# Expert results in attention's output banks, the early placing one turn sooner, and VectorE's division product and choice in the next turn

## The chip, the cores and the metric

The kernel runs on one core of a Trainium2 chip. Five engines work there side by side, each on its own queue of instructions in order: PE (TensorE, matrix products into PSUM), DVE (VectorE), ACT (ScalarE), POOL (GpSimd) and SP (SyncE, which here only issues DMAs). An instruction waits on semaphores for what other engines must have done first, and while it waits, everything behind it in its queue waits too. The metric is the device time of one execution in microseconds (us); the median of three runs of the kernel before is 878.63.

## The reference, cut to what matters

Attention by clusters, and on its output a layer of experts. A query may see only the keys whose nearest centroid is its own; each token then goes to one of 8 experts.

```python
q_assign = argmax(q_n @ c_n.T);  k_assign = argmax(k_n @ c_n.T)   # 4 x 8 heads, 768 rows of 64
scores = where(q_assign == k_assign, q @ k.T / 8, -1e9)
attn = softmax(scores) @ v                       # -> x, 3072 tokens x 512
expert_idx = argmax(x_n @ emb_n.T / tau)         # 8 experts
out = gate * (relu(x @ w1[e]) @ w2[e])           # w1 512x1024, w2 1024x512, all float32
```

## The kernel before, in words

**Attention.** The work goes over 16 pairs of heads (four batches, four pairs each). A pair has 12 units (2 halves of the queries, 6 blocks of 128 keys) and is done in six turns, numbered `it` 0 to 5, of two units each. In a turn PE first makes the scores (`s_ps`, L353) of the next two units and ACT takes their exponentials (`prob`, L364); then come small pieces of work for the pair after it, or for the routing of a finished batch (`between`, L796); then PE multiplies the probabilities of this turn's two units with v into `o_ps` (L373), and DVE adds them into `acc` (L382, L392). Six units make a group with one `o_ps` and one `acc`. A turn after a group's last unit, that is at `it` 0 and 3, `total` has PE sum `acc` over the keys (L400) and ACT copy the sum to `den`; `divide` has DVE take the reciprocal (L416) and multiply `o_ps` by it into `xT` (L417).

The mask is made for the next pair: at `it` 2 `assign` finds each row's largest centroid product (`amax`, `sel`), POOL weighs `sel` (L276), and `choose` makes of it the one-hot rows `oh` (`pm` L282, `oh` L283). At `it` 4 PE turns these, and DVE copies the queries' part to `qH` (L302), ACT the keys' part to `kH`. The next pair's scores, from `it` 5 on, read both.

**Experts.** Tokens are sorted by expert into blocks of 128 rows. The first four blocks are placed early, from the first three batches, while the last batch's attention runs: `Places` works in the steps `ranks`, `firsts`, `experts`, `dest`, `hot_blocks`, `hot_rows` and `tokens`, and the table `early` (L780) says in which turn each is done; `(3, 4)` is `it` 4 of the batch's last pair. After `tokens`, POOL gathers a block's rows (`fetch`, L693, an indirect DMA into `xin`). A block j is then done in three steps: `turn_x` (PE transposes into `x_ps`, L723, copied to `xTm` by ACT or DVE, L725), `hidden` (PE into `h_ps`, L737, ACT to `hT`, L744) and `result` (PE into `y_ps`, L753, ACT scales it to `y`, L763, POOL scatters it to the output, L764). `weights` has SP load an expert's two matrices where the expert changes.

**Order.** Attention and the first blocks are in `manual_schedule`: PE, DVE and ACT do there what the program says, in its order. The loop over the later blocks (L921) is ordered by the framework, which puts one product of block j's `result` between the transposes of block j+1 and that block's `hidden`. PSUM has eight banks: two for `o_ps`, two for `misc`, four for `s_ps`; these four become one `x_ps`, two `h_ps` and one `y_ps` when attention is over.

Of the kernel before, what the change touches and what calls it, by code (L numbers as in the profile page):

```python
# [9 lines left out]
F32 = mybir.dt.float32  # L10
# [8 lines left out]
P = 128  # L19
# [18 lines left out]
def kernel(  # L38
# [83 lines left out]
    ldp = at.enter_context(tc.tile_pool(name="ldp", bufs=2, side="right"))  # L122
    trp = at.enter_context(tc.tile_pool(name="trp", bufs=2, side="right"))
    pp = at.enter_context(tc.tile_pool(name="pp", bufs=5, side="right"))
    psS = at.enter_context(tc.tile_pool(name="psS", bufs=2, space=PSUM, side="right"))

# [98 lines left out]
    def prep_pieces(n):  # L227
# [89 lines left out]
        def mean(bk):  # L317
# [12 lines left out]
            "turn1": lambda: (turn("q", 1), turn("k", 1)),  # L330
            "values": values,
            "products": products,
            "assign": lambda: (assign(), choose()),
            "hots": lambda: (turn_hot(0, "q"), turn_hot(1, "k")),
        }

# [1 line left out]
    GU = NJ  # L338
# [56 lines left out]
    def total(g):  # L395

        d = gr[g]
        bk = misc()
        for h in range(2):
            nc.tensor.matmul(  # L400
                bk[D * h : D * h + D, 0:HS],
                lhsT=ones,
                rhs=d["acc"][:, h],
                start=True,
                stop=True,
            )
        d["den"] = smp.tile([P, HS], F32, tag="den", name="den")
        nc.scalar.copy(d["den"], bk[:, 0:HS])  # L408

    def divide(g):  # L410
        n, hq, _ = units[GU * g]
        b, hp = pairs[n]
        d = gr[g]
        if (b, hq) not in xT:
            xT[b, hq] = xp.tile([P, NHP, HS], F32, tag="xT", name="xT", bufs=3)
        nc.vector.reciprocal(d["den"], d["den"])  # L416
        nc.vector.scalar_tensor_tensor(  # L417
            out=xT[b, hq][:, hp],
            in0=d["o_ps"][:, 0:HS],
            scalar=ld[n]["ev"],  # L420
            in1=d["den"],
            op0=ALU.add,
            op1=ALU.mult,
        )
        d.clear()
# [290 lines left out]
            cond=c > 0,  # L716
        )

    def turn_x(j, evict):
        d = mo[j]  # L720
        bk = psX.tile([P, DM], F32, tag="x_ps", name="x_ps")
        for c in range(KD):
            nc.tensor.transpose(bk[:, P * c : P * c + P], d["xin"][:, P * c : P * c + P], ident)  # L723
        d["xT"] = mop.tile([P, DM], F32, tag="xTm", name="xTm")
        evict(d["xT"], bk)  # L725

    def hidden(j, halves=(0, 1)):
# [18 lines left out]
    def result(j, halves=(0, 1)):  # L746
        d = mo[j]
        for half in halves:
            if half == 0:
                d["y_ps"] = psY.tile([P, DM], F32, tag="y_ps", name="y_ps")  # L750
            bk = d["y_ps"]
            for c in range(KF // 2 * half, KF // 2 * half + KF // 2):
                nc.tensor.matmul(  # L753
                    bk,
                    lhsT=d["hT"][:, P * c : P * c + P],
                    rhs=w2s[j % 2][:, c],
                    start=(c == 0),
                    stop=(c == KF - 1),
                )
            if half == 1:  # L760
                to = gidxs[0][:, j : j + 1] if j < KA else sidx[:, j - KA : j - KA + 1]
                y = mop.tile([P, DM], F32, tag="y", name="y", bufs=3)
                nc.scalar.activation(y, bk, ACTF.Copy, scale=d["xin"][:, DM : DM + 1])  # L763
                nc.gpsimd.indirect_dma_start(  # L764
                    out=out[:],
                    out_offset=bass.IndirectOffsetOnAxis(ap=to, axis=0),
                    in_=y,
                    in_offset=None,
                    bounds_check=N - 1,
                    oob_is_err=False,  # L770
                )
                del mo[j]
# [6 lines left out]
    pa = Places(0, rta)  # L779
    early = {  # L780
        (2, 3): lambda: pa.ranks(),
        (2, 5): lambda: (pa.firsts(), pa.experts()),
        (3, 0): lambda: pa.dest(),
        (3, 1): lambda: (pa.hot_blocks(), pa.hot_rows(0, 3)),
        (3, 2): lambda: pa.hot_rows(1, 3),
        (3, 3): lambda: pa.hot_rows(2, 3),
        (3, 4): lambda: (pa.tokens(), fetch(0), fetch(1), fetch(2)),
    }

    def piece(n, name):  # L790
# [5 lines left out]
    def between(n, it):  # L796
        b, nb = divmod(n, NHP)
        if it == 5:
            piece(n + 2, "turn0")
            if n + 1 == NP:  # L800
                route[b] = route_pieces(b)
                rows(2 * n)
                route[b][0](0)
        elif it == 0:
            piece(n + 1, "turn1" if n else "turn0")
        elif it == 1:
            piece(n + 1, "values")
            piece(n + 1, "products")
            if n > 0:
                rows(2 * n - 2)  # L810
        elif it == 2:
            piece(n + 1, "assign")
            if n > 0:
                rows(2 * n - 1)
        elif it == 4:
            piece(n + 1, "hots")
        if b > 0:
            if nb == 0 and it == 3:
                route[b - 1] = route_pieces(b - 1)
                for half in range(2):  # L820
                    route[b - 1][0](half)
            j = NJ * nb + it - 3
            if 0 <= j < NJ:
                route[b - 1][2](j)
            if nb == 1 and it == 3:
                for half in range(2):
                    route[b - 1][1](half)
            if nb in (1, 2) and 0 <= j - NJ < 4:
                route[b - 1][3][j - NJ]()
        if b == B - 1 and (nb, it) in early:  # L830
            early[nb, it]()
        if b == B - 1 and (nb, it) == (3, 0):
            weights(0)
            weights(1)

    with tc.manual_schedule(engines={EngineType.PE, EngineType.DVE, EngineType.Activation}):
        for name in ("turn0", "turn1", "values", "products", "assign", "hots"):
            piece(0, name)
        load(1, "qk")
        for m in range(2):  # L840
            scores(m)
            expo(m)
        for i in range(0, len(units), 2):
            n, it = divmod(i // 2, NJ)
            if it == 0 and n + 1 < NP:
                load(n + 1, "v")
            if it == 4 and n + 2 < NP:
                load(n + 2, "qk")
            if it == 0 and n == 1:

                for w in range(2):
                    nc.sync.dma_start(
                        out=w1s[w], in_=moe_w1[0].rearrange("(c p) f -> p c f", p=P)
                    )
                    nc.sync.dma_start(
                        out=w2s[w], in_=moe_w2[0].rearrange("(c p) d -> p c d", p=P)
                    )
            for m in range(i + 2, min(i + 4, len(units))):
                scores(m)
                expo(m)  # L860
            between(n, it)
            for m in range(i, i + 2):
                attend(m)
            if i % GU == 0 and i > 0:
                total(i // GU - 1)
                divide(i // GU - 1)
            if i == 0:
                piece(1, "turn1")
        at.close()
        tile_waits = {"side": "right", "reuse_waits": "tile"}  # L870
        mop = ctx.enter_context(tc.tile_pool(name="mop", bufs=2, **tile_waits))
        rtb = ctx.enter_context(tc.tile_pool(name="rtb", bufs=1, **tile_waits))
        psX, psH, psY = (
            ctx.enter_context(tc.tile_pool(name=name, bufs=bufs, space=PSUM, **tile_waits))
            for name, bufs in (("psX", 1), ("psH", 2), ("psY", 1))
        )

        products, logits, norms, (choose, *gates) = route[B - 1]
        pb = Places(1, rtb)
        turn_x(0, nc.scalar.copy)  # L880
        hidden(0, (0,))
        total(ngroups - 1)
        divide(ngroups - 1)
        for j in range(NJ // 2):
            norms(j)
        hidden(0, (1,))
        turn_x(1, nc.scalar.copy)
        logits(0)
        rows(ngroups - 1)
        products(1)  # L890
        hidden(1, (0,))
        for j in range(NJ // 2, NJ):
            norms(j)
        logits(1)
        choose()
        hidden(1, (1,))
        for gate in gates:
            gate()
        fetch(3)
        turn_x(2, nc.scalar.copy)  # L900
        result(0, (0,))
        pb.ranks()
        pb.firsts()
        result(0, (1,))
        weights(2)
        pb.dest()
        pb.experts()
        hidden(2)
        pb.hot_blocks()
        turn_x(3, nc.scalar.copy)  # L910
        pb.hot_rows(0, 1)
        result(1)
        weights(3)
        hidden(3, (0,))
        pb.tokens()
        hidden(3, (1,))
# [72 lines left out]
```

## Time and profile before

| | |
|---|---|
| runs | 878.63 us median (878.53 to 878.80) |
| profiled execution | 881.44 us, span 879.6 us, clock granted to PE 0.989 of full speed |
| PE | busy 834.4 us, 95% of the span |
| DVE / ACT / POOL | 357.2 / 305.2 / 117.4 us busy |
| attention | until about 440 us of the span |
| experts | from there to 870 us, 28 blocks; a block takes 15.06 us |

PE is hardly ever idle, so what counts is what PE waits for; the other engines' idle time means nothing by itself. A bracket at a row's end gives the idle time of that engine just before the row, and what ended it. PE's matmuls of float32 stand in the trace as two records each (x4 for two matmuls), and their ends are modelled: from start to start is the safer measure.

### The profile page before, as it was taken

Reading aid. Unit: us, or ns where it says so; the run is one execution under the profiler, and the core shown is the slowest. Engines: PE = TensorE matmul, PEld = TensorE weight load, DVE = VectorE, ACT = ScalarE, POOL = GpSimd, SP = SyncE. Lnnn points to the kernel's source line nnn. Section 1 sums busy time; section 2 is a strip of 40 time slices with the busy share of each in tenths; the row PEclk is TensorE's granted clock in tenths of the full one; section 3 lists DMA queues with packets and bytes.
Section 4 is the critical chain, followed back from the end, with each engine's and each line's share of the span. In section 5 each row is a group of like instructions: output and inputs, shape, how many; then the busy total and the mean of one; then the engine's idle time right before and its main releaser. Section 6 shows DMA issues by size and latency. Waiting matters only on the chain.

```text
span 879.6 us, 12823 instructions
## 1 busy us (share of the span) xinstructions
PE 834.4 (95%) x5227; PEld 496.4 (56%) x5227; DVE 357.2 (41%) x521; ACT 305.2 (35%) x489; POOL 117.4 (13%) x172
## 2 busy tenths in 40 slices
PE   4999999999999999999989999999999999999995
PEld 2444444444444444444376676767676767767672
DVE  3477777777778777788925000000000000000000
ACT  3455555755566545665432111111111111111110
POOL 4010101210102111111011101011010101010100
PEclk8899999999999999999999999999999999999998
DMA  9922201242201422001037756838383847216400
GB/s 239 324 55 55 53 19 37 56 126 55 54 19 37 126 54 55 19 19 73 1 132 272 275 195 231 303 128 322 120 314 136 290 160 271 86 61 241 173 29 21
DMA packets 108781, 115.24 MB, mean 131 GB/s; under 512 B 77221, under 2 KB 77221, under 8 KB 108208
## 3 DMA queue, kind: packets, MB, share of 16 engines
q1 hardware_dynamic: 104064, 100.68, 35.6%
q0 software_dynamic: 4480, 13.65, 4.1%
q8 instruction: 43, 0.70, 0.3%
q14 instruction: 18, 0.15, 0.1%
q10 hardware_dynamic: 176, 0.05, 0.0%
HBM read 152.11 MB, written 13.64 MB: 188 GB/s over the span
## 4 chain that ended last, share of the span: by engine, by line
PE 32%; issue 31%; DMA 21%; DVE 12%; POOL 2%; ACT 1%; SPq 0%; POOLq 0%; DVEq 0%
DMA out_dram<-y,sidx 16%; PE s_ps L353 13%; PE o_ps L373 8%; DVE den L416 4%; PE misc L238 3%; DMA out_dram<-y,gidx 3%; DVE acc L392 2%; PE misc L400 2%; PE h_ps L737 2%; POOL sel L276 1%; PE misc L253 1%; DMA xin<-x_rows,gidx 1%; DVE xT L417 1%; PE misc L434 1%; PE misc L266 1%
## 5 line engine op out<-in xcount | busy, mean ns | idle before, releaser
L737 PEld LDWEIGHTS h_ps<-xTm,w1s 128*128 128x128 f32 x1792 | 205.9, 193 | 15.2 <-DVE xTm L725 7.2
L753 PE MATMUL y_ps<-w2s,hT 128*128 128x512 f32 x448 | 203.6, 598 | 8.9 <-ACT y L763 8.9
L737 PE MATMUL h_ps<-xTm,w1s 128*128 128x128 f32 x1792 | 207.2, 277 | 0.7 <-ACT xTm L725 0.7
L364 ACT ACTIVATE prob<-s_ps 128x768 f32<-128x768 f32 x192 | 154.6, 811 | 140.6 <-PE s_ps L353 81.4
L353 PE MATMUL s_ps<-qT,kT 64*128 64x384 f32 x768 | 157.8, 489 | 0.0
L725 DVE COPY xTm<-x_ps 128x512 f32<-128x512 f32 x24 | 16.6, 692 | 340.8 <-PE x_ps L723 340.8
L373 PE MATMUL o_ps<-prob,v 128*64 128x384 f32 x768 | 145.1, 499 | 0.0
L753 PEld LDWEIGHTS y_ps<-w2s,hT 128*128 128x128 f32 x448 | 81.0, 190 | 97.2 <-issue 81.7
L392 DVE TENSOR_TENSOR acc<-acc,prob 128x768 f32<-128x768 f32 x128 | 122.1, 954 | 3.6
L744 ACT ACTIVATE hT<-h_ps 128x512 f32<-128x512 f32 x56 | 33.4, 597 | 209.2 <-PE h_ps L737 209.2
L416 DVE RECIPROCAL den<-den 128x384 f32<-128x384 f32 x32 | 81.7, 2552 | 33.1 <-ACT den L408 33.1
L353 PEld LDWEIGHTS s_ps<-qT,kT 64*128 64x128 f32 x768 | 70.1, 192 | 21.9 <-issue 21.9
L373 PEld LDWEIGHTS o_ps<-prob,v 128*64 128x64 f32 x768 | 46.6, 136 | 54.4 <-issue 53.4
L763 ACT ACTIVATE y<-y_ps,xin 128x512 f32<-128x512 f32 x28 | 19.2, 687 | 154.8 <-PE y_ps L753 142.6
L353 PE MATMUL s_ps<-qH,kH 64*128 64x384 bf16 x384 | 64.6, 331 | 6.5 <-DVE qH L302 5.3
L764 POOL DMA_INDIRECT out_dram<-y,sidx x24 | 24.0, 1001 | 300.8 <-ACT y L763 293.9
L353 PEld LDWEIGHTS <-kH 64*128 64x128 bf16 x384 | 20.6, 94 | 75.5 <-issue 52.9
L312 POOL TENSOR_TENSOR vs<-v 128x384 f32<-128x384 f32 x16 | 16.5, 1030 | 222.1 <-DMA v<-in_v_dram 222.1
L693 POOL DMA_INDIRECT xin<-x_rows,gidx x28 | 30.2, 1078 | 31.4 <-issue 11.2
L247 DVE COPY kT<-misc 128x384 f32<-128x384 f32 x32 | 17.8, 558 | 40.6 <-PE misc L238 40.2
L400 PE MATMUL misc<-acc,ones 128*64 128x384 f32 x128 | 26.7, 493 | 4.9 <-DVE acc L392 4.9
L382 DVE SCALAR_TENSOR_TENSOR acc<-prob 128x768 f32<-128x768 f32 x32 | 30.3, 948 | 0.0
(183 smaller groups left out, 487.2 us busy)
## 6 DMA issues: line engine op xcount, KB each, us to landing
w1s<-in_moe_w_dram SPq DMA_DIRECT2D x30, 2048.0 KB
w2s<-in_moe_w_dram SPq DMA_DIRECT2D x30, 2048.0 KB
x_rows<-xr SPq DMA_DIRECT2D x4, 1539.0 KB
q<-in_q_dram SPq DMA_DIRECT2D x32, 192.0 KB
k<-in_k_dram SPq DMA_DIRECT2D x32, 192.0 KB
v<-in_v_dram SPq DMA_DIRECT2D x32, 192.0 KB
xin<-x_rows,gidx POOLq DMA_INDIRECT x28, 7.2
out_dram<-y,sidx POOLq DMA_INDIRECT x24, 6.9
```

The lines of the kernel that those rows point to most:

```text
L238: nc.tensor.transpose(bk[:, P * j : P * j + P], t[nm][:, NJ // 2 * half + j].rearrange("p h d -> p (h d)"), ident,)
L353: nc.tensor.matmul(s_ps[:, h, 0:HS], lhsT=t[l][rows, P * j : P * j + P], rhs=t[r][rows, HS * hq : HS * hq + HS], start=first, stop=not first,)
L364: nc.scalar.activation(d["prob"], d["s_ps"][:, :, 0:HS], ACTF.Exp)
L373: nc.tensor.matmul(g["o_ps"][D * h : D * h + D, 0:HS], lhsT=ld[n]["v"][:, j, h], rhs=d["prob"][:, h], start=(j == 0), stop=(j == NJ - 1),)
L382: nc.vector.scalar_tensor_tensor(out=g["acc"], in0=un[i - 1]["prob"], scalar=NJ * EPS, in1=d["prob"], op0=ALU.add, op1=ALU.add,)
L392: nc.vector.tensor_tensor(g["acc"], g["acc"], d["prob"], ALU.add)
L400: nc.tensor.matmul(bk[D * h : D * h + D, 0:HS], lhsT=ones, rhs=d["acc"][:, h], start=True, stop=True,)
L416: nc.vector.reciprocal(d["den"], d["den"])
L693: nc.gpsimd.indirect_dma_start(out=xin, out_offset=None, in_=x_rows[0:n], in_offset=bass.IndirectOffsetOnAxis(ap=gidxs[part][:, c : c + 1] ...
L737: nc.tensor.matmul(bk[:, m : m + P], lhsT=w1s[j % 2][:, c, f0 + m : f0 + m + P], rhs=d["xT"][:, P * c : P * c + P], start=(c == 0), stop=( ...
L744: nc.scalar.activation(d["hT"][:, f0 : f0 + 512], bk, ACTF.Relu)
L753: nc.tensor.matmul(bk, lhsT=d["hT"][:, P * c : P * c + P], rhs=w2s[j % 2][:, c], start=(c == 0), stop=(c == KF - 1),)
```

## The change

Four things are moved.

The results go into the two `o_ps` banks, which attention has left by then, in turns; `y_ps` has no bank of its own, and `h_ps` gets three. For that `psS` is closed one turn earlier, and the transposes of block 0 move ahead of attention's last two units, with `xTm` in a buffer of `acc`.

The reciprocal moves from `divide` to `total`, where it comes as before, and the rest of `divide` moves to the next turn, behind that turn's pieces and ahead of its additions. `choose` moves from `it` 2 to `it` 3. The early steps from `firsts` on come a turn sooner. In block 1's `result` the transposes of block 3 move between its two halves.

```diff
-            "assign": lambda: (assign(), choose()),
+            "assign": assign,
+            "choose": choose,
...
         nc.scalar.copy(d["den"], bk[:, 0:HS])
+        nc.vector.reciprocal(d["den"], d["den"])
...
-        nc.vector.reciprocal(d["den"], d["den"])
...
-                d["y_ps"] = psY.tile([P, DM], F32, tag="y_ps", name="y_ps")
+                d["y_ps"] = psO.tile([P, DM], F32, tag="o_ps", name="y_ps")
...
-        (2, 5): lambda: (pa.firsts(), pa.experts()),
-        (3, 0): lambda: pa.dest(),
...
-        (3, 4): lambda: (pa.tokens(), fetch(0), fetch(1), fetch(2)),
+        (2, 4): lambda: (pa.firsts(), pa.experts()),
+        (2, 5): lambda: pa.dest(),
...
+        (3, 3): lambda: (pa.tokens(), fetch(0), fetch(1), fetch(2)),
...
+        elif it == 3:
+            piece(n + 1, "choose")
...
             between(n, it)
+            if i % GU == 2 and i > GU:
+                divide(i // GU - 1)
+            if i + 2 == len(units):
+                ats.close()
...
+                turn_x(0, nc.scalar.copy, xp.tile([P, DM], F32, tag="acc", name="xTm"))
...
                 total(i // GU - 1)
-                divide(i // GU - 1)
...
-        turn_x(0, nc.scalar.copy)
...
+        pb.hot_rows(0, 1)
+        result(1, (0,))
         turn_x(3, nc.scalar.copy)
-        pb.hot_rows(0, 1)
-        result(1)
+        result(1, (1,))
```

On DVE, in a pair of the first batch, `it` 2 to 4 stood in this order before (`acc` x2 are a turn's two additions):

```order
L274 TENSOR_REDUCE amax<-misc 128x24
L275 TENSOR_TENSOR sel<-misc,amax 128x384
L282 TENSOR_REDUCE pm<-sel 128x24
L283 TENSOR_TENSOR oh_176<-sel,pm 128x24x16
L392 TENSOR_TENSOR acc<-acc,prob 128x768 x2
L382 SCALAR_TENSOR_TENSOR acc<-prob 128x768
L416 RECIPROCAL den<-den 128x384
L417 SCALAR_TENSOR_TENSOR xT<-o_ps,ev,den 128x384
L302 TENSOR_SCALAR qH<-misc 128x768
L306 COPY ev<-misc 128x1
```

And there now:

```order
L275 TENSOR_REDUCE amax<-misc 128x24
L276 TENSOR_TENSOR sel<-misc,amax 128x384
L394 TENSOR_TENSOR acc<-acc,prob 128x768 x2
L283 TENSOR_REDUCE pm<-sel 128x24
L284 TENSOR_TENSOR oh_176<-sel,pm 128x24x16
L384 SCALAR_TENSOR_TENSOR acc<-prob 128x768
L411 RECIPROCAL den<-den 128x384
L303 TENSOR_SCALAR qH<-misc 128x768
L307 COPY ev<-misc 128x1
L419 SCALAR_TENSOR_TENSOR xT<-o_ps,ev,den 128x384
```

The two additions have moved ahead of the choice, and the product `xT` behind `qH`.

On DVE too, the end of the step `dest` in the last batch and what followed it, before:

```order
L637 CAST blka<-blkfa 128x18
L638 SCALAR_TENSOR_TENSOR loa<-blkfa,desta 128x18
L382 SCALAR_TENSOR_TENSOR acc<-prob 128x768
L416 RECIPROCAL den<-den 128x384
L417 SCALAR_TENSOR_TENSOR xT<-o_ps,ev,den 128x384
```

And now:

```order
L639 CAST blka<-blkfa 128x18
L640 SCALAR_TENSOR_TENSOR loa<-blkfa,desta 128x18
L394 TENSOR_TENSOR acc<-acc,prob 128x768 x2
L650 TENSOR_TENSOR bma<-io_b,blka 128x72
L652 TENSOR_TENSOR rra<-bma,tok_hi 128x18x4
```

The two additions that complete a group's `acc`, which were ahead of all of `dest`, now stand behind it.

On PE, the last turn of attention and the first block, before:

```order
L434 MATMUL misc<-ident,xT 128x128 x3
L456 MATMUL misc<-xT,embT 32x384 x4
L373 MATMUL o_ps<-prob,v_3584 64x384 x4
L723 MATMUL x_ps<-ident,xin 128x128 x4
L737 MATMUL h_ps<-xTm,w1s_58 128x128 x16
```

And now:

```order
L436 MATMUL misc<-ident,xT 128x128 x3
L458 MATMUL misc<-xT,embT 32x384 x4
L725 MATMUL x_ps<-ident,xin 128x128 x4
L375 MATMUL o_ps<-prob,v_3584 64x384 x4
L739 MATMUL h_ps<-xTm,w1s_58 128x128 x16
```

The transposes `x_ps` have moved ahead of the last products with v. In the loop over blocks PE's order is the same as before; the banks alone differ.

## Rows read from the trace of the kernel before

**Rows 1.** The page: busy us, share of the span and instructions, by engine

```profile
PE 834.4 (95%) x5227; PEld 496.4 (56%) x5227; DVE 357.2 (41%) x521; ACT 305.2 (35%) x489; POOL 117.4 (13%) x172
```

**Rows 2.** PE's waits over the whole span: us in total, times, longest

```profile
PE y_ps L753 <- ACT y L763: 8.9, 25, 0.8
PE s_ps L353 <- DVE qH L302: 5.3, 15, 0.8
PE misc L400 <- DVE acc L392: 4.9, 10, 0.7
PE x_ps L723 <- DMA xin<-x_rows,gidx: 3.1, 2, 2.0
```

**Rows 3.** Timeline of PE, half a pair: start us, us, instruction, idle before

```profile
222.55 1.51 PE L373 MATMUL o_ps<-prob,v 128*64 128x384 f32 x8
224.56 0.87 PE L400 MATMUL misc<-acc,ones 128*64 128x384 f32 x4 [0.50 <-DVE acc L392]
225.36 0.34 PE L353 MATMUL s_ps<-qH,kH 64*128 64x384 bf16 x2
...
229.78 0.34 PE L353 MATMUL s_ps<-qH,kH 64*128 64x384 bf16 x2 [0.24 <-DVE qH L302]
...
236.28 1.51 PE L373 MATMUL o_ps<-prob,v 128*64 128x384 f32 x8
...
238.36 0.34 PE L353 MATMUL s_ps<-qH,kH 64*128 64x384 bf16 x2
```

**Rows 4.** Timeline of DVE, the same pair and the next one's choice

```profile
225.98 2.55 DVE L416 RECIPROCAL den<-den 128x384 f32<-128x384 f32 x1 [0.69 <-ACT den L408]
228.65 0.62 DVE L417 SCALAR_TENSOR_TENSOR xT<-o_ps,ev,den 128x384 f32<-128x384 f32 x1
229.18 0.55 DVE L302 TENSOR_SCALAR qH<-misc 128x768 bf16<-128x768 bf16 x1
...
247.26 0.55 DVE L282 TENSOR_REDUCE pm<-sel 128x24 bf16<-128x384 bf16 x1 [1.02 <-POOL sel L276]
...
248.33 2.01 DVE L392 TENSOR_TENSOR acc<-acc,prob 128x768 f32<-128x768 f32 x2
```

**Rows 5.** Timeline of PE, a turn of the loop over blocks

```profile
621.53 0.60 PE L723 MATMUL x_ps<-ident,xin 128*128 128x128 f32 x4
622.47 1.13 PE L753 MATMUL y_ps<-w2s,hT 128*128 128x512 f32 x2 [0.34 <-ACT y L763]
623.43 7.31 PE L737 MATMUL h_ps<-xTm,w1s 128*128 128x128 f32 x64
630.58 6.17 PE L753 MATMUL y_ps<-w2s,hT 128*128 128x512 f32 x14
```

**Rows 6.** Timeline of DVE, the same turn

```profile
622.17 0.69 DVE L725 COPY xTm<-x_ps 128x512 f32<-128x512 f32 x1 [14.37 <-PE x_ps L723]
```

**Rows 7.** Timeline of DVE, additions, first of the twelve of `dest`, next after them

```profile
417.44 1.93 DVE L392 TENSOR_TENSOR acc<-acc,prob 128x768 f32<-128x768 f32 x2
419.29 0.30 DVE L614 TENSOR_TENSOR wa<-rka,offa 128x144 f32<-128x144 f32 x1
...
422.09 0.95 DVE L382 SCALAR_TENSOR_TENSOR acc<-prob 128x768 f32<-128x768 f32 x1
```

**Rows 8.** Timeline of PE, the last pair and the first block

```profile
420.05 0.81 PE L400 MATMUL misc<-acc,ones 128*64 128x384 f32 x4
...
442.08 0.63 PE L723 MATMUL x_ps<-ident,xin 128*128 128x128 f32 x4 [1.98 <-DMA xin<-x_rows,gidx]
443.39 5.37 PE L737 MATMUL h_ps<-xTm,w1s 128*128 128x128 f32 x32 [0.68 <-ACT xTm L725]
...
449.48 3.84 PE L737 MATMUL h_ps<-xTm,w1s 128*128 128x128 f32 x32
```

**Rows 9.** Timeline of POOL, the first gather

```profile
437.97 1.67 POOL L693 DMA_INDIRECT xin<-x_rows,gidx  x1 [11.17 <-DVE gidx L678]
```

**Rows 10.** Stretches: us, busy time by engine, granted clock of PE, DMA share, GB/s

```profile
443.40:445.00 1.60, 1.60 (x7) 1.60 (x8) 0.00 (x0) 0.00 (x0) 0.00 (x0) 0.50 0.55 169
```

More of the change, by code (lines that the diff above doesn't have):

```diff
@@ L124 @@
     pp = at.enter_context(tc.tile_pool(name="pp", bufs=5, side="right"))
-    psS = at.enter_context(tc.tile_pool(name="psS", bufs=2, space=PSUM, side="right"))
+    ats = ctx.enter_context(ExitStack())
+    psS = ats.enter_context(tc.tile_pool(name="psS", bufs=2, space=PSUM, side="right"))
     def misc():
@@ L717, in weights, with turn_x @@
         )
-    def turn_x(j, evict):
+    def turn_x(j, evict, xT=None):
         d = mo[j]
@@ L723, in turn_x @@
             nc.tensor.transpose(bk[:, P * c : P * c + P], d["xin"][:, P * c : P * c + P], ident)
-        d["xT"] = mop.tile([P, DM], F32, tag="xTm", name="xTm")
+        d["xT"] = mop.tile([P, DM], F32, tag="xTm", name="xTm") if xT is None else xT
         evict(d["xT"], bk)
@@ L781 @@
         (2, 3): lambda: pa.ranks(),
-        (2, 5): lambda: (pa.firsts(), pa.experts()),
-        (3, 0): lambda: pa.dest(),
-        (3, 1): lambda: (pa.hot_blocks(), pa.hot_rows(0, 3)),
-        (3, 2): lambda: pa.hot_rows(1, 3),
-        (3, 3): lambda: pa.hot_rows(2, 3),
-        (3, 4): lambda: (pa.tokens(), fetch(0), fetch(1), fetch(2)),
+        (2, 4): lambda: (pa.firsts(), pa.experts()),
+        (2, 5): lambda: pa.dest(),
+        (3, 0): lambda: (pa.hot_blocks(), pa.hot_rows(0, 3)),
+        (3, 1): lambda: pa.hot_rows(1, 3),
+        (3, 2): lambda: pa.hot_rows(2, 3),
+        (3, 3): lambda: (pa.tokens(), fetch(0), fetch(1), fetch(2)),
     }
@@ L836 @@
     with tc.manual_schedule(engines={EngineType.PE, EngineType.DVE, EngineType.Activation}):
-        for name in ("turn0", "turn1", "values", "products", "assign", "hots"):
+        for name in ("turn0", "turn1", "values", "products", "assign", "choose", "hots"):
             piece(0, name)
@@ L861 @@
             between(n, it)
+            if i % GU == 2 and i > GU:
+                divide(i // GU - 1)
+            if i + 2 == len(units):
+                ats.close()
+                tile_waits = {"side": "right", "reuse_waits": "tile"}
+                psX = ctx.enter_context(tc.tile_pool(name="psX", bufs=1, space=PSUM, **tile_waits))
+                turn_x(0, nc.scalar.copy, xp.tile([P, DM], F32, tag="acc", name="xTm"))
             for m in range(i, i + 2):
@@ L869 @@
         at.close()
-        tile_waits = {"side": "right", "reuse_waits": "tile"}
         mop = ctx.enter_context(tc.tile_pool(name="mop", bufs=2, **tile_waits))
         rtb = ctx.enter_context(tc.tile_pool(name="rtb", bufs=1, **tile_waits))
[L873 to L876, printed above, removed]
+        psH = ctx.enter_context(tc.tile_pool(name="psH", bufs=3, space=PSUM, **tile_waits))
         products, logits, norms, (choose, *gates) = route[B - 1]
         pb = Places(1, rtb)
-        turn_x(0, nc.scalar.copy)
         hidden(0, (0,))
```

## The prediction

> **What bounds the kernel now.** I read the page first [rows 1]: PE is busy for 834.4 of 879.6 us, so time can come only from PE's idle 45 us and from PE working slowly. Next the list of PE's waits [rows 2]. Four of its lines are touched by the change: results waiting for ACT's copy of the result before (8.9 us), scores waiting for `qH` (5.3), sums waiting for `acc` (4.9), transposes waiting for a gather (3.1); 22.2 us in all. The reader should see that these are many small waits, of 0.24 to 0.8, in every pair and every block. Then the timelines, to see what a wait costs beside its idle time and what is late next: a pair [rows 3, 4], a turn of the loop [rows 5, 6], and the passage from attention to the experts [rows 7 to 10].
>
> The sum is made against the profiled execution's own 881.44 us, which is 2.8 above the median of 878.63; I take each gain off either.
>
> **Attention.** The instructions are the same; DVE's order changes.
>
> At `it` 2 the additions stood behind the choice, and that behind POOL's product: DVE sat 1.02 us idle before `pm`, and the choice's `pm` and `oh` take 1.07, from 247.26 to 248.33 [rows 4]. With the additions ahead of them, they end 2.1 us sooner. PE's sum L400 waited 0.5 for them [rows 3], 0.7 at most [rows 2]. So all ten of these waits go. A wait of 0.50 costs more than that: from the products at 222.55 to the next scores at 225.36 it is 2.81 us, without the wait 2.08 (236.28 to 238.36), so 0.73, of which 0.23 is PE starting again. Ten times: 4.9 + 2.3 = 7.2 us.
>
> The choice now stands in the turn of the reciprocal. That costs nothing while DVE reaches the reciprocal before `den` does: there is 0.69 idle before the reciprocal [rows 4], and DVE comes 1.02 sooner, because the wait for POOL is now filled with additions. PE comes 0.73 sooner, which leaves about 1.0 of slack. PE reads `oh` only at `it` 4, behind that turn's scores.
>
> `qH` stood behind the product `xT`, which takes 0.53 from start to next start (228.65 to 229.18 [rows 4]). It now comes first, 0.53 sooner against waits that average 0.24 in most pairs (the 229.78 row of [rows 3] is one). In the few with 0.8, where the routing fills DVE, 0.53 is not enough by itself, but part of POOL's 1.02 comes on top. All 5.3 go; I add nothing for starting again. The product comes after `qH`, a turn before PE turns `xT`, so nobody waits for it in a plain pair; the `o_ps` bank that it frees is written again two turns on. Attention: 7.2 + 5.3 = 12.5 us. From below: 9, if another copy (`kH` by ACT stands at the same gate) is late in some pairs; from above 13.5, if each `qH` wait cost 0.07 more.
>
> **The loop over blocks.** In each turn PE does four transposes, one product of the last block's result and then `hidden`. That product waits 0.34 for ACT to empty the one bank; with two banks the other has been empty for a whole turn. From transposes to `hidden` it is 1.90 us (621.53 to 623.43 [rows 5]). What is late next? First the product itself: it could start at 0.94 - 0.34 = 0.60 after the transposes, and its two records take 0.44 each (6.17 us for 14), so it ends at 1.48. Then `xTm`: DVE's copy ends at 622.17 + 0.69, which is 1.33 after the transposes' start [rows 6]; add some 0.15 until PE has taken it, an estimate from the 0.1 that PE loses on starting again in [rows 5] (0.96 from the product's start to `hidden`, against 0.88). Both come out at 1.48 to 1.49, so 0.41 a turn. The 25 waits are 24 of 0.34 and one of 0.8: 24 x 0.41 = 9.8 us, and 0.8 for the last block, where nothing follows but its own result. From below 24 x 0.2 = 4.8, if PE takes `xTm` as late as 1.7; from above 24 x 0.5 = 12, if neither is felt.
>
> The Trainium skill speaks against this term: its page "TensorE: Matmul & The Clock Gate", section "HAM oscillation — how this bites in real kernels", reports of a matmul kernel that "Adding PSUM double-buffering gave no further gain". By it the loop would give 0 in place of 10.6, and the sum would be 15.2. The row bears the other way: here the bank is the wait that ends last, 0.34 each time.
>
> **The passage.** Before, PE stood 1.98 us for the first gather and 0.68 for `xTm`, and then ran half of `hidden` in 5.37 us in place of 3.84, the granted clock being at its lower level, 0.50 (1.2 of 2.4 GHz) [rows 8, 10]. The gather is issued at 437.97 and lands with the transposes' start at 442.08 [rows 9, 8]. Its whole chain now comes a turn sooner (4.4 us from 225.36 to 229.78 [rows 3]), past no other work of POOL or SP, and `xTm` is copied beside the last products with v. So 1.98 + 0.68 + 1.53 = 4.2 us would go.
>
> Against that stands a new wait. The two additions that complete a group now come behind the twelve instructions of `dest`, 2.80 us (419.29 to 422.09 [rows 7]). They ended at 419.29; they will end there + 2.80, less what DVE is ahead by then (0 to 1.0 of POOL's wait; I take 0.35, because the reciprocal between is held by `den`): about 421.75. PE's L400 stood at 420.05 [rows 8]; it comes sooner by the waits gone ahead of it in this pair, 0.4 to 1.0 by their kinds in [rows 2, 3]; I take 0.65, so 419.4. PE waits 2.35 there, and 0.23 for starting again: 2.6 us (1.7 to 3.3). Behind L400 on PE are the next scores, so ACT's exponentials and DVE's reciprocal come later too; DVE is the fuller engine here, and the transposes of the last `xT` may wait some 0.7 for the product that now comes a turn later. Short waits of that size leave in this stretch too; I let them cancel. If the clock falls after the new wait as it did after the old ones, another 1.5 is lost; I don't count it, but the range does. Passage: 4.2 - 2.6 = 1.6 us, from -0.5 to 4.2.
>
> **Block 3.** The second gather wait is 3.1 - 1.98 = 1.1 us [rows 2, 8]; half of block 1's result now stands ahead of the transposes, eight records of 0.44, so the gather is hidden. 1.1 us; 0 if the weights that SP loads for block 3 are late instead.
>
> Three `h_ps` banks in place of two: nothing; the list of PE's waits has none for `h_ps` to be emptied.
>
> **The sum.** 12.5 + 9.8 + 0.8 + 1.6 + 1.1 = 25.8 us: 855.6 for an execution like the profiled one, 852.8 for the median.
>
> **The rivals.**
>
> *The loop gives nothing.* `hidden` can't start before `xTm`, and the product was beside DVE's copy anyway; or the product's start still waits for ACT, for `hT`. For: copy and product end within 0.1 of each other. Against: today `hidden` starts 0.57 after the copy's end (1.33 to 1.90), so the copy does not set it; and `hT` was copied a turn earlier. Time: 852.8 + 10.6 = 863.4.
>
> *Attention gives half.* DVE's work is the same, and PE, coming sooner, meets `kH` or the exponentials late. For: `prob` has five buffers that DVE's additions free. Against: additions come sooner, not later. Time: 852.8 + 6.2 = 859.0.
>
> *Slower: the choice holds up the reciprocal in every pair.* If the additions at `it` 2 didn't come sooner, 1.07 us of choice would stand between them and the reciprocal, and `qH` would be later by as much. Then the sum loses attention's 12.5, and 1.07 x 16 = 17 more is spent, and the passage's 1.6 goes: 25.8 - 12.5 - 17 - 1.6 = -5.3, so 884. It decides from where attention loses (9.8 + 0.8 + 1.1) / 16 = 0.73 us a pair. Against: the reciprocal has 0.69 of idle time ahead of it today, and the additions read probabilities made a turn before.
>
> *It doesn't do what it says.* The sums then wait for something else at the same time, and the loop for `xTm` as long as for the bank: 878.
>
> **How the numbers follow.** Forecast 0.79, its own range 848 to 859. Loop nothing 0.10, attention half 0.06, slower 0.03, no change 0.02. The lows of the terms together (9 + 4.8 + 0.8 - 0.5 + 0) give 864.5, the highs (13.5 + 12 + 1 + 4.2 + 1.1) 846.8; all ends together are unlikely, but the first rival lies near the low one: 847 to 863. A measurement here tells 0.2% (1.8 us) from no change. Faster: 0.95; same 0.02; slower 0.03.
>
> **What would show it.** Right: no waits of L400 for `acc` but one, of 1.4 to 3 us, in the turn after `dest`; none of scores for `qH` or under 0.2 in some pairs; loop turns of 14.65 us in place of 15.06, with `hidden` waiting for DVE's `xTm`; no wait for a gather at either place; the first half of `hidden` in 3.8 us. Wrong: turns of 15.06, `qH` waits that grow, or a long stretch at the granted clock 0.50 after the new wait, which would make the passage a loss.

## The result and the profile after

The changed kernel takes 856.77 us (median of four runs, 855.87 to 857.99), against 878.71 of the kernel before beside it: a ratio of 0.9745, interval 0.9725 to 0.9766. The forecast was 852.8, its range 847 to 863. The profiled execution took 857.06 us, its span 855.3. Lines have moved: L353 is now L355, L392 L394, L400 L402, L417 L419, L434 L436, L723 L725, L737 L739, L753 L755; the reciprocal is L411.

The page's busy row, against [rows 1], and the list of PE's waits, against [rows 2]:

```profile
PE 828.1 (97%) x5227; PEld 491.2 (57%) x5227; DVE 362.5 (42%) x521; ACT 305.5 (36%) x489; POOL 126.5 (15%) x172
```

```profile
PE h_ps L739 <- DMA w1s<-in_moe_w_dram: 2.8, 5, 0.7
PE misc L402 <- DVE acc L394: 2.2, 1, 2.2
...
PE misc L436 <- DVE xT L419: 0.7, 1, 0.7
```

All four lines of [rows 2] are gone, but for one wait of L402. Two lines are new: `hidden` waits five times for the load of w1, and one transpose waits for `xT`. DVE and POOL are busier with the same instructions.

PE in the half pair of [rows 3], and DVE's reciprocal in it, as [rows 4]:

```profile
214.98 1.51 PE L375 MATMUL o_ps<-prob,v 128*64 128x384 f32 x8
216.32 0.82 PE L402 MATMUL misc<-acc,ones 128*64 128x384 f32 x4
217.06 0.34 PE L355 MATMUL s_ps<-qH,kH 64*128 64x384 bf16 x2
...
221.17 0.34 PE L355 MATMUL s_ps<-qH,kH 64*128 64x384 bf16 x2
```

```profile
217.69 2.55 DVE L411 RECIPROCAL den<-den 128x384 f32<-128x384 f32 x1 [0.57 <-ACT den L410]
```

From products to the next scores it is now 2.08 us (2.81 before), and neither the sum nor the scores at 221.17 wait. DVE still reaches the reciprocal 0.57 before `den` does.

PE in two turns of the loop, as [rows 5], and DVE in the first:

```profile
618.63 0.60 PE L725 MATMUL x_ps<-ident,xin 128*128 128x128 f32 x4
619.07 1.02 PE L755 MATMUL y_ps<-w2s,hT 128*128 128x512 f32 x2
620.02 7.41 PE L739 MATMUL h_ps<-xTm,w1s 128*128 128x128 f32 x64
627.27 6.17 PE L755 MATMUL y_ps<-w2s,hT 128*128 128x512 f32 x14
633.28 0.60 PE L725 MATMUL x_ps<-ident,xin 128*128 128x128 f32 x4
633.71 1.02 PE L755 MATMUL y_ps<-w2s,hT 128*128 128x512 f32 x2
635.33 7.38 PE L739 MATMUL h_ps<-xTm,w1s 128*128 128x128 f32 x64 [0.59 <-DMA w1s<-in_moe_w_dram]
```

```profile
619.27 0.69 DVE L727 COPY xTm<-x_ps 128x512 f32<-128x512 f32 x1 [13.95 <-PE x_ps L725]
```

A turn takes 14.65 (618.63 to 633.28; 15.06 before): the product follows the transposes after 0.44 and `hidden` after 1.39 (620.02), not 1.90, 0.06 behind the end of DVE's copy (619.96). From the start of `hidden` to that of `result` it is 7.25 (7.15 before), so 0.10 of the 0.51 goes again. In the next turn `hidden` comes after 2.05, because w1 is late.

DVE and PE behind `dest`, against [rows 7, 8]:

```profile
403.96 0.30 DVE L616 TENSOR_TENSOR wa<-rka,offa 128x144 f32<-128x144 f32 x1
...
406.75 1.95 DVE L394 TENSOR_TENSOR acc<-acc,prob 128x768 f32<-128x768 f32 x2
```

```profile
408.75 0.87 PE L402 MATMUL misc<-acc,ones 128*64 128x384 f32 x4 [2.17 <-DVE acc L394]
409.55 0.34 PE L355 MATMUL s_ps<-qH,kH 64*128 64x384 bf16 x2
409.73 1.37 PE L355 MATMUL s_ps<-qT,kT 64*128 64x384 f32 x4
...
429.99 3.84 PE L739 MATMUL h_ps<-xTm,w1s 128*128 128x128 f32 x32
```

And the stretch behind that wait, columns as [rows 10]:

```profile
409.60:413.30 3.70, 3.70 (x17) 1.67 (x15) 3.70 (x3) 1.84 (x3) 0.00 (x0) 0.54 0.00 0
```

PE waits 2.17, and then the granted clock falls to its lower level (1.2 of 2.4 GHz; 0.54 is the mean of this stretch, the fall included): the scores at 409.73 take 1.37 where 0.81 is usual. `hidden`'s first half takes 3.84, no longer 5.37 [rows 8].

**Where the time came from.** PE's instructions are the same in all kernels here, so I cut each profiled execution at the starts of the same five of them: the first, the 27th and the last of the 32 sums of `acc`, the transposes of block 4, and the span's end. Differences of two starts in the PE timeline, us:

| kernel | head | attention, pairs 1 to 13 | passage | blocks 0 to 3 | loop | span |
|---|---|---|---|---|---|---|
| before | 41.71 | 340.61 | 66.37 | 52.15 | 378.76 | 879.6 |
| changed | 39.83 | 330.33 | 63.60 | 51.60 | 369.94 | 855.3 |
| changed, second profile | 40.16 | 330.33 | 61.95 | 51.75 | 369.51 | 853.7 |
| b_choose | 39.83 | 334.37 | 66.85 | 52.00 | 378.55 | 871.6 |
| b_divide | 40.77 | 335.75 | 62.78 | 52.56 | 378.64 | 870.5 |
| b_attn | 39.43 | 330.33 | 62.20 | 52.20 | 378.54 | 862.7 |
| b_loop | 41.65 | 340.66 | 66.36 | 52.37 | 370.16 | 871.2 |
| a_place | 39.84 | 330.34 | 62.20 | 51.75 | 369.57 | 853.7 |
| a_tab | 40.57 | 330.33 | 64.57 | 51.91 | 369.22 | 856.6 |
| a_dest | 39.59 | 330.33 | 63.66 | 51.80 | 370.52 | 855.9 |
| a_w1 | 40.29 | 330.33 | 63.54 | 50.81 | 367.43 | 852.4 |
| a_dest_w1 | 39.92 | 330.33 | 62.03 | 50.81 | 367.51 | 850.6 |
| a_best | 40.22 | 330.33 | 62.38 | 50.81 | 367.46 | 851.2 |
| a_pool | 38.62 | 330.33 | 63.60 | 51.85 | 369.30 | 853.7 |

Before to changed: 1.9 + 10.3 + 2.8 + 0.55 + 8.8 = 24.3 us. Between kernels with the same order there, attention's column differs by 0.05 at most, so it says what a median can't; the head (38.6 to 40.6 with attention changed) and the loop with its waits for w1 (369.2 to 370.5) repeat less well.

### The profile page after: what moved, and what is told of

Read it like the earlier page. It is cut to its first block, busy times and chain, and to the rows that moved or that the text cites. A ratio compares the mean times of both kernels' runs of the same rounds, so it can differ in the third digit from the quotient of the medians.

```text
span 855.3 us, 12807 instructions
## 1 busy us (share of the span) xinstructions
PE 828.1 (97%) x5227; PEld 491.2 (57%) x5227; DVE 362.5 (42%) x521; ACT 305.5 (36%) x489; POOL 126.5 (15%) x172
## 4 chain that ended last, share of the span: by engine, by line
PE 49%; issue 25%; DMA 22%; DVE 2%; SPq 0%; POOL 0%; ACT 0%; POOLq 0%
PE s_ps L355 19%; DMA out_dram<-y,sidx 17%; PE o_ps L375 16%; PE misc L239 3%; DMA out_dram<-y,gidx 3%; PE misc L402 2%; PE h_ps L739 2%; DMA w1s<-in_moe_w_dram 2%; PE misc L436 2%; PE misc L297 1%; PE misc L254 1%; PE misc L267 1%; PE y_ps L755 1%; PE misc L458 1%; DVE den L411 1%
## 5 line engine op out<-in xcount | busy, mean ns | idle before, releaser
L739 PEld LDWEIGHTS h_ps<-xTm,w1s 128*128 128x128 f32 x1792 | 202.5, 192 | 24.2 <-DVE xTm L727 20.5
L739 PE MATMUL h_ps<-xTm,w1s 128*128 128x128 f32 x1792 | 207.9, 277 | 2.8 <-DMA w1s<-in_moe_w_dram 2.8
L755 PE MATMUL y_ps<-w2s,hT 128*128 128x512 f32 x448 | 201.1, 592 | 0.0
L355 PE MATMUL s_ps<-qT,kT 64*128 64x384 f32 x768 | 157.7, 489 | 0.0
L394 DVE TENSOR_TENSOR acc<-acc,prob 128x768 f32<-128x768 f32 x128 | 129.8, 1014 | 3.6
L755 PEld LDWEIGHTS y_ps<-w2s,hT 128*128 128x128 f32 x448 | 81.0, 190 | 81.8 <-issue 81.8
L411 DVE RECIPROCAL den<-den 128x384 f32<-128x384 f32 x32 | 81.7, 2552 | 31.2 <-ACT den L410 31.2
L355 PEld LDWEIGHTS s_ps<-qT,kT 64*128 64x128 f32 x768 | 69.6, 191 | 22.1 <-issue 22.1
L355 PE MATMUL s_ps<-qH,kH 64*128 64x384 bf16 x384 | 64.1, 331 | 1.0 <-ACT kH L306 0.9
L355 PEld LDWEIGHTS <-kH 64*128 64x128 bf16 x384 | 19.0, 94 | 70.8 <-issue 48.2
L277 POOL TENSOR_TENSOR sel<-sel,prefc 128x384 bf16<-128x384 bf16 x16 | 24.2, 1514 | 110.2 <-DVE sel L276 110.2
```

The costliest lines, as they stand in the source:

```text
L277: nc.gpsimd.tensor_tensor(sel, sel, bc(prefc, shp, 1), ALU.mult)
L355: nc.tensor.matmul(s_ps[:, h, 0:HS], lhsT=t[l][rows, P * j : P * j + P], rhs=t[r][rows, HS * hq : HS * hq + HS], start=first, stop=not first,)
L394: nc.vector.tensor_tensor(g["acc"], g["acc"], d["prob"], ALU.add)
L739: nc.tensor.matmul(bk[:, m : m + P], lhsT=w1s[j % 2][:, c, f0 + m : f0 + m + P], rhs=d["xT"][:, P * c : P * c + P], start=(c == 0), stop=( ...
L755: nc.tensor.matmul(bk, lhsT=d["hT"][:, P * c : P * c + P], rhs=w2s[j % 2][:, c], start=(c == 0), stop=(c == KF - 1),)
```

## The experiments

**One part alone, on the kernel before.** `b_loop`: the banks of the results.

```diff
-                d["y_ps"] = psY.tile([P, DM], F32, tag="y_ps", name="y_ps")
+                d["y_ps"] = psO.tile([P, DM], F32, tag="o_ps", name="y_ps")
...
-            for name, bufs in (("psX", 1), ("psH", 2), ("psY", 1))
+            for name, bufs in (("psX", 1), ("psH", 3))
```

> The kernel before with one part of the change alone: the results go into attention's two output banks, and h_ps has three. Theory (the loop's new bound is the weight loads): each turn saves 0.41 us (24 x 0.41 = 9.8) and the last block 0.8, and four turns that follow two weight loads give back 0.66 each, 2.6: 8.0 us, about 870.7; the list of PE's waits has four of hidden for w1s, of 0.3 to 0.7. Rival 1 (the weight waits of the changed kernel come from the other parts): 10.6 us, 868.1, no such waits. Rival 2 (the loop gives nothing): 878.7.

872.14 us against 881.17, ratio 0.9902 (0.9886 to 0.9917); the loop column falls by 8.6. PE's list:

```profile
PE h_ps L737 <- DMA w1s<-in_moe_w_dram: 2.5, 5, 0.7
```

The waits for weights come with the shorter turn, not with the other parts. Five of them, not four: block 4 waits here too (0.38), where in the changed kernel block 3 does. The third `h_ps` bank came along and wasn't run apart; PE's list of before has no wait for `h_ps` to be emptied.

`b_attn` has all of attention's part, `b_choose` the first of these two edits, `b_divide` the second:

```diff
-            "assign": lambda: (assign(), choose()),
+            "assign": assign,
+            "choose": choose,
...
+        elif it == 3:
+            piece(n + 1, "choose")
...
```

```diff
         nc.scalar.copy(d["den"], bk[:, 0:HS])
+        nc.vector.reciprocal(d["den"], d["den"])
...
+            if i % GU == 2 and i > GU:
+                divide(i // GU - 1)
...
-                divide(i // GU - 1)
```

> The kernel before with attention's part of the change alone: the choice in the next turn, the reciprocal in total, the product xT in the next turn; places, transposes and results as before. Theory: the ten waits of sums for acc (7.2 us) and the fifteen of scores for qH (5.3 us) go, 12.5 us: 866.2. Rival (part of it comes from the early placing): 10 us or less, over 868.5, with waits for qH or acc left in the last batch.

> The kernel before with only the choice moved from it 2 to it 3. Theory: the ten waits for acc go with what PE loses on starting again, 7.2 us: 871.5; the fifteen waits for qH stay as they are, 5.3 us. Rival (starting again costs nothing, only the idle time comes back): 4.9 us, 873.8. Rival (the choice delays the reciprocal): the waits for qH grow to 10 us or more, gain under 3 us.

> The kernel before with only division changed: reciprocal in total, product xT in the next turn. Theory: the fifteen waits for qH go, 5.3 us and nothing for starting again: 873.4; the ten waits for acc stay, 4.9 us. Rival (each such wait costs 0.07 to 0.23 more than its idle time, as the waits for acc did): 6.4 to 8.8 us, 870 to 872.3. Rival (the product ahead of the additions delays the sums): waits for acc grow by 0.5 each, no gain.

Measured: 865.58 (0.9829, 0.9816 to 0.9843), 872.95 (0.9912, 0.9898 to 0.9925), 872.26 (0.9906, 0.9892 to 0.9920), all against 881.17: 15.1, 7.8 and 8.3 us by the ratios (15.6, 8.2 and 8.9 from median to median). The lists of PE's waits, of `b_choose` and of `b_divide`:

```profile
PE s_ps L354 <- DVE qH L302: 3.3, 14, 0.3
PE x_ps L724 <- DMA xin<-x_rows,gidx: 3.0, 2, 2.0
...
PE misc L401 <- DVE acc L393: 0.4, 1, 0.4
```

```profile
PE misc L400 <- DVE acc L392: 4.5, 9, 0.7
...
PE x_ps L723 <- DMA xin<-x_rows,gidx: 2.2, 2, 1.6
PE misc L434 <- DVE xT L417: 1.9, 2, 1.4
```

Each edit removes its own waits. In pairs 1 to 13 there are seven waits for `acc` behind the first sum and thirteen for `qH` (3.5 and 4.3 us). The choice's edit gains 6.24 there: 3.5, 1.1 of the `qH` waits, and 1.6 for starting again, 0.23 a wait. Division's gains 4.86, 0.04 a wait above the idle time. So `acc` waits cost 0.23 more than they show, `qH` waits hardly anything, as the prediction had it. `b_attn` gains more than 12.5 for a reason that wasn't in the expectation: the passage column falls by 4.17, and `b_divide` alone does 3.59 of it. Its gather waits 0.64 instead of 1.98 and the first half of `hidden` takes 3.84, with the old table:

```profile
434.23 0.63 PE L723 MATMUL x_ps<-ident,xin 128*128 128x128 f32 x4 [0.64 <-DMA xin<-x_rows,gidx]
435.54 3.84 PE L737 MATMUL h_ps<-xTm,w1s 128*128 128x128 f32 x32 [0.68 <-ACT xTm L725]
```

(The 1.6 in its list is the second gather, of block 3.) `b_choose` leaves the first gather's wait as it was (2.0), and its passage column is 0.48 longer than before: that half of `hidden` takes 6.79 there, nearly all of it at the lower clock.

**The passage edits.** `a_dest`: the changed kernel with `dest` behind its turn's additions.

```diff
-        (2, 5): lambda: pa.dest(),
...
             for m in range(i, i + 2):
                 attend(m)
+            if (n, it) == (NP - 2, 5):
+                pa.dest()
```

> The changed kernel once more, as the measure for the three beside it: 856.8.

> The changed kernel with the step dest behind its turn's two additions instead of ahead of them; all else as it is. Theory A (the new wait and the fall of the clock behind it are a matter of order): the 2.2 us wait of the sums goes with the 0.17 of starting again, and the 1.7 us by which the rows after it (408.75 to 414.83, against 420.05 to 424.44 before) run longer at the lower clock: 4.0 us, 852.8. Theory B (DVE, which is busy without a gap from 399.8 to 417, bounds the whole stretch): PE runs ahead and waits for DVE's reciprocal, products or additions a turn later instead; gain of 0 to 1.5 us, 855.3 to 856.8.

The changed kernel again: 856.89. `a_dest`: 857.71 (855.11 to 858.23), no gain. Theory B: the wait of L402 is gone (it starts at 406.17), and two others are there. PE of `a_dest`:

```profile
411.84 0.34 PE L355 MATMUL s_ps<-qH,kH 64*128 64x384 bf16 x2 [0.30 <-ACT prob L366]
...
414.74 0.55 PE L436 MATMUL misc<-ident,xT 128*128 128x128 f32 x3 [1.91 <-DVE xT L419]
415.21 1.92 PE L375 MATMUL o_ps<-prob,v 128*64 128x384 f32 x8
```

2.2 us of waits out, 2.2 in (and the clock fell behind the new one in this execution). DVE works without a gap here (399 to 419 us in the changed kernel); its order only chooses which of PE's instructions waits.

`a_place` takes both passage edits back (table and block 0's transposes), `a_tab` the table alone.

```diff
-        (2, 4): lambda: (pa.firsts(), pa.experts()),
-        (2, 5): lambda: pa.dest(),
+        (2, 5): lambda: (pa.firsts(), pa.experts()),
+        (3, 0): lambda: pa.dest(),
...
-                turn_x(0, nc.scalar.copy, xp.tile([P, DM], F32, tag="acc", name="xTm"))
...
+        turn_x(0, nc.scalar.copy)
         hidden(0, (0,))
```

> The changed kernel without its passage part: the table of early steps as before (dest at it 0 of the last pair, gather at it 4) and block 0's transposes behind the last products with v; attention, banks and block 3 as changed. Theory C (the moves in attention already bring the gather in time, and the early table only adds the wait behind dest): with attention's part alone the first half of hidden starts at 428.2, in the changed kernel at 428.7 or, where the clock falls, 430.0: 0.5 to 1.8 us faster than it, 855.1 to 856.4. The prediction's sum (the passage as changed earns 1.6): 858.5. Were the passage's 4.2 us of waits all back: 861.

> The changed kernel with the early table of before alone; block 0's transposes stay ahead of the last products with v. Theory (the early table is there for the early transposes: without it they stand for the gather 1.45 us sooner, and the products behind them stand too): the gather's wait is 0.6 + 1.45 = 2.05 us, the wait for xTm is none, and from the 27th sum of acc to the last one is 62.9 us, against 62.2 with late transposes, and 1.5 more if the clock falls behind the wait: 856.4 to 858. Rival (the two halves of the passage part are independent, the early transposes earn 0.68): 61.5 us there, 855.0.

`a_place` 855.72 (0.9723, 0.9710 to 0.9736), `a_tab` 858.14 (0.9752, 0.9738 to 0.9765): the first as expected, the second 0.1 above its theory's range and 3 above its rival. PE of `a_tab`:

```profile
428.09 0.63 PE L725 MATMUL x_ps<-ident,xin 128*128 128x128 f32 x4 [2.09 <-DMA xin<-x_rows,gidx]
430.84 4.70 PE L739 MATMUL h_ps<-xTm,w1s 128*128 128x128 f32 x32
```

The passage column: 62.20 with neither edit, 64.57 with the early transposes alone, 61.95 or 63.60 with both. Theory C holds: together the two edits earn nothing that can be measured (+0.25 to -1.4 us, by whether the clock falls). The early table is what the early transposes need; the table with late transposes was not run.

**The weight loads.** `a_w1`: w1 is issued when `hidden` has left its buffer, ahead of the w2 load that waits for a result.

```diff
             hidden(j + 1)
+        if j + 3 < usual:
+            weights(j + 3, (1,))
         result(j)
         if j + 2 < usual:
-            weights(j + 2)
+            weights(j + 2, (2,))
...
```

Blocks 2 to 4 are treated alike ahead of the loop.

> The changed kernel with each w1 load issued as soon as hidden has left its buffer, ahead of the w2 load of the block before it in SP's order; the same bytes are moved. Theory (SP's order holds the load back: w1s stands behind a w2 load that waits for a result): the five waits of hidden for w1s go, 5 x 0.66 = 3.3 us: 853.5. Rival (the loads are bound by bandwidth, two of 2 MB in a turn): the waits stay, 856.8. Rival (the waits are late releases and not late data): the waits stay but shorter.

> The changed kernel with both edits, dest behind the additions and the w1 loads ahead. Theory: the two are in different stretches and add: 4.0 + 3.3 = 7.3 us, 849.5. By theory B for dest: 852 to 853.5.

853.19 (0.9684, 0.9669 to 0.9700), 3.7 under the changed kernel beside it. `a_dest_w1`: 854.84 (0.9702; runs from 852.4 to 855.3), above both expectations and no better than `a_w1`, so `dest` earns nothing here either. No wait for w1 is left in the two; blocks 0 to 3 take 50.81 and the loop 367.4, 0.8 and 2.1 to 2.5 less. SP's queue, in the changed kernel and in `a_w1`:

```profile
618.83 0.38 SPq L715 DMA_DIRECT2D w2s<-in_moe_w_dram  x1
619.54 0.37 SPq L710 DMA_DIRECT2D w1s<-in_moe_w_dram  x1
```

```profile
611.05 0.37 SPq L711 DMA_DIRECT2D w1s<-in_moe_w_dram  x1
617.06 0.37 SPq L717 DMA_DIRECT2D w2s<-in_moe_w_dram  x1
```

w1 goes 6 us earlier than w2, with the same bytes. Bandwidth had its part: the DMA engines of the changed kernel between issue and release (last two columns: DMA share, GB/s) are full.

```profile
620.00:622.00 2.00, 2.00 (x18) 1.98 (x18) 0.00 (x0) 0.00 (x0) 1.70 (x2) 1.00 0.90 210
...
630.00:632.00 2.00, 2.00 (x7) 0.80 (x6) 0.00 (x0) 0.00 (x0) 0.00 (x0) 1.00 1.04 424
632.00:634.00 2.00, 2.00 (x9) 1.15 (x8) 0.09 (x1) 0.52 (x1) 0.00 (x0) 1.00 0.42 166
```

Two loads at once fill them for some 13 us, and PE is let go 16.7 us after the transposes beside which they were issued (618.63 to 635.33). Before, it was due there after 15.06 + 1.90 = 16.96; now after 14.64 + 1.39 = 16.03. The 0.26 of slack was less than the 0.93 that the change took.

**The best of both.** `a_best` is `a_place` with `a_w1`'s loads, and at `it` 1 the product `xT` ahead of that turn's early steps:

```diff
+            if it == 1 and n > 0:
+                divide(i // GU - 1)
             between(n, it)
-            if i % GU == 2 and i > GU:
+            if it == 4:
                 divide(i // GU - 1)
```

> The changed kernel with the table and transposes of before, with w1 loads ahead of w2 loads, and with the division's product at it 1 ahead of that turn's early steps instead of behind them. Theory C and the theory of the loads add: 853.2 less 0.5 to 1.8, and less the 1.4 us that PE waits for xT behind hot_rows where attention's part is alone: 850 to 851.3. Rival (DVE bounds the stretch, the wait moves to the sums or to the gather): 851.4 to 853.

852.97 (0.9688, 0.9675 to 0.9701): better than the changed kernel, the same as `a_w1`. The rival was right: the passage column is 62.38, no less than `a_place`'s 62.20; the 1.4 us wait for `xT` became 0.2, and waits for `prob` (0.3) and `acc` (0.4) came instead.

**POOL beside DVE.** `a_pool`:

```diff
-            nc.gpsimd.tensor_tensor(sel, sel, bc(prefc, shp, 1), ALU.mult)
+            nc.vector.tensor_tensor(sel, sel, bc(prefc, shp, 1), ALU.mult)
```

> The changed kernel with POOL's product sel given to DVE, ahead of the additions. In the changed kernel POOL's product and DVE's additions run at the same time and both are long (two additions 2.5 us beside it against 1.9 to 2.0 elsewhere; the product 1.5 us against 0.9 before). Theory (they slow each other): the two additions of it 2 take 1.95 in all pairs. Rival (the additions are longer for another cause, where they stand or what they read): 2.5 us still. Time: 856.8 by both, since PE waits for neither.

855.99 us. DVE's additions grouped by line, of the changed kernel and of `a_pool` (busy us, mean ns | idle before), and POOL's product in the former:

```profile
L394 DVE TENSOR_TENSOR acc<-acc,prob 128x768 f32<-128x768 f32 x128 | 129.8, 1014 | 3.6
...
L277 POOL TENSOR_TENSOR sel<-sel,prefc 128x384 bf16<-128x384 bf16 x16 | 24.2, 1514 | 110.2 <-DVE sel L276 110.2
```

```profile
L394 DVE TENSOR_TENSOR acc<-acc,prob 128x768 f32<-128x768 f32 x128 | 122.0, 953 | 3.6
```

The additions are back at their length of before without POOL beside them: they slowed each other.

## Why the prediction was right, and where not

**Attention, 12.5 us: right, by its own steps.** Pairs 1 to 13 gave 10.3, where its prices make 9.5 (seven times 0.51 + 0.23, and 4.3 for `qH`). The head gave 1.9 more; about 0.9 is the first wait for `acc` (0.74 and starting again), and the other 1.0 stands before it: the granted clock is 1.00 from 24.1 us on, where before it was 0.50 until 26.8, so that scores took 1.49 in place of 0.81. The heads of kernels with attention changed differ as much among themselves, so I don't count it to the change.

**The loop, 9.8 + 0.8: the step that failed.** The turn is 14.64 to 14.65, forecast 14.65: `hidden` starts 0.10 sooner than forecast (1.39 for 1.49) and takes 0.10 longer, and as forecast it starts with the end of DVE's copy. `a_w1`'s loop, with no other wait left, is 11.3 us under that of before, forecast 10.6. What the term left out is that a turn has a deadline in it: where two weight loads are issued together, a turn was 0.26 us longer than they need. Four such turns in the loop give back 2.1 to 2.5 (0.5 to 0.6 each), so the loop gave 8.8. The Trainium skill's page "TensorE: Matmul & The Clock Gate", section "HAM oscillation — how this bites in real kernels", reports of a matmul kernel that double-buffering PSUM gave no further gain; that result doesn't carry over to this kernel, where it gave 0.41 us a turn.

**Block 3, 1.1 us: half.** The gather's wait went; `hidden` of block 3 then waited 0.56 for w1, which the prediction named as its condition for 0, and 0.55 is left. With `a_w1`'s loads it is 1.34. No run has this edit alone; without it the gather's wait stays, 1.2 in `b_attn`.

**The passage, 1.6 us: the size came out by luck, the reason didn't.** The column holds besides it attention's last waits (two for `acc`, two for `qH`), which the same prices make 2.1; 3.7 together, measured 2.8 with the fall of the clock and 4.4 without. The new wait was 2.17, forecast 2.35. The clock did fall behind it in one profile of two, 1.65 us, which the range held. But the 4.2 us were put down to the early table and transposes, and `b_divide` brings 3.6 in this column with neither: where DVE's product, 0.53 us, no longer stands ahead of the token copies, the gather waits 0.6. (That accounts for part of it: from POOL's issue to the transposes the gather also takes 3.76 instead of 4.11, and the rest isn't taken apart.) Against `a_place` the early table and transposes give 0.25 at best, and where the clock falls they lose 1.4, as the prediction's last sign had it. What stood against it, a wait on a full DVE, comes in every order tried here: 1.4 to 2.2 us in one place, or in `a_best` 0.2 to 0.45 in three.

**The sum.** Terms of 25.8 against 24.3 by the two profiled executions; 1.8 is missing in the loop and 0.55 in block 3. The median is off by more, 4.0 us, because the sum was taken off the medians: the profiled execution of before was 2.8 above its own, that of the changed kernel 0.3 above. In the later comparisons the kernel before had medians of 879.8 to 881.2, so 878.63 was at the low end of what it does.

None of the rivals came: the loop gave most of its term, and the reciprocal kept its place, with 0.57 of slack in the pair shown where the prediction counted on about 1.0: the two additions ahead of the choice now take 2.53 instead of 1.94 (last section), which is more than the difference.

## What to carry to other kernels

Before a turn is made shorter, look up what must be done within it without PE, loads above all, and subtract: the slack is in the trace of before. Where two edits can each remove a wait, price the second with the first already in; here the second half of the change had little left to remove. On an engine that has no gap, moving work only moves the wait; a queue's order is worth changing where a transfer stands behind something that waits longer.

## What the runs showed that was not expected

DVE's float32 addition and POOL's bf16 product slow each other: two additions take 2.5 us instead of 1.9 to 2.0, the product 1.51 instead of 0.91. Over the kernel that is 7.7 us of DVE, all of it hidden. After waits of 1.9 to 2.2 us the granted clock fell in some executions of a kernel and not in others (63.54 to 63.66 against 61.95 to 62.03 us for the same passage). After waits of 1.6 us and less in the passage and in the blocks it didn't in any of these profiles.
